# Out-projection of seven batches by seven block products on pairs of token chunks, in an attention and mixture kernel

## The chip, the cores and the metric

One core of a Trainium2 chip. The time is the device time of one execution in microseconds (us), and a median is over the runs of one kernel on one chip. All runs told here are fast: the granted TensorE clock was 0.95 to 1.0 as a mean over the run. The profile is of one of these executions; its span is some 2 us shorter than the timed value.

## The reference

```python
def sm_attn(qq, kk, vv):                       # softmax attention, 8 heads of 64
    s = scale * np.matmul(qq, kk.transpose(0, 1, 3, 2))
    ...
    return np.matmul(a, vv)
p_packed = sm_attn(p, k, v)                    # 32 packed queries per head
x = sm_attn(q, p_packed, p_packed)             # 8 batches x 576 tokens x 512
h = x @ w_in                                   # 512 x 2048
out = (h * np.cos(h)) @ w_out                  # 2048 x 512: the out-projection
```

## The kernel before

The kernel works batch by batch. A batch has a short *head* (scores, softmax sums, normalising to `a2n`) and a long *slot* of sixteen hidden blocks `h_mm`, which make `gT`. The out-projection of the batch before is the *filler*: its matmuls are handed out in small portions between the other work of TensorE (`fill(n)`). A batch has four chunks of 128 tokens, and what is left of two batches makes one joint chunk. Names used below: a *bank* is a piece of the memory that TensorE writes its results to, and another engine has to empty it before TensorE can use it again; `vp` is a batch's `v`, reordered by one copy on GpSimd; `PPW` is the packed attention result times `w_in`, which VectorE or ScalarE casts out of its banks; `rs` is a scaling of two numbers per partition on VectorE that the softmax needs.

```python
def h_mm(b, fc):
    ...                                   # 4 matmuls of 288 columns into one psA buffer (of 3)
    ACT.activation(out=csv, in_=ps, func=AF.Sin, bias=PI_HALF)
    V.tensor_tensor(out=gT..., in0=ps, in1=csv, op=ALU.mult)
    ...                                   # fc 7 and 15: GpSimd copies the rest tokens to `joint`

def out_gen(b):                           # one chunk = 16 matmuls of 512 columns into one bank
    groups = [(0, 1), (2,), (3,)] if b == 0 else [(c,) for c in range(n_chunks(b))]
    for grp in groups:
        pss = {c: O.tile([128, DM], FP32, name="ot", tag="ot") for c in grp}   # two banks
        ...
                    w = joint[b // 2][:, fc, :] if c == 4 else gT[b][:, fc, c * 128:(c + 1) * 128]
                    nc.tensor.matmul(pss[c], w, w_out_bf[:, fc, :], ...)
                    if fc == NFC - 1:
                        copy(out_eng[...], osb, pss[c])       # VectorE or ScalarE, then the store
```

The softmax here doesn't subtract the row's maximum and nothing guards it: scores larger than these inputs give would overflow.

## Time and profile before

| | before |
|---|---|
| time, median of 4 runs | 248.2 us (248.0 to 248.84) |
| span of the profiled run | 246.8 us |
| TensorE / VectorE / ScalarE / GpSimd busy | 94% / 67% / 68% / 23% |
| heads of batches 3 to 7 | 8.6 to 8.8 us |
| slots of batches 3 to 6 | 16.6 to 19.6 us |

The stages are cut at ScalarE's table loads: it loads the exponential's table when a head begins and the sine's when a slot begins. The lines themselves are in the prediction below. What to take from them is that TensorE has hardly an idle moment from the first batch on, and that no other engine is near its limit.

### The profile page before, as it was taken

How to read it: one execution, taken by the hardware profiler on the slowest of the kernel's cores; microseconds unless marked ns; L12 is line 12 of the kernel's file. 1: busy time of each engine (PE TensorE's matmuls, PEld its weight loads, DVE VectorE, ACT ScalarE, POOL GpSimd, SP SyncE). 2: the span in 40 equal slices, each digit the busy share in tenths (PEclk: the TensorE clock that was granted, in tenths of full speed). 3: DMA queues.
4: the chain of work that ended last, by engine and by line, in shares of the span. 5: the costliest groups of instructions: out<-in, count | busy, mean ns of one | idle time of the engine just before them, and what ended most of it. 6: DMA issues, size and time to landing. Idle time of an engine off the chain costs nothing.

```text
span 246.8 us, 5023 instructions
## 1 busy us (share of the span) xinstructions
PE 233.2 (94%) x1996; PEld 130.9 (53%) x2029; DVE 165.2 (67%) x248; ACT 169.0 (68%) x282; POOL 57.7 (23%) x70
## 2 busy tenths in 40 slices
PE   8788799999999999999999999999999999999993
PEld 3454374566545654565446554565456554665452
DVE  3549987677658776678767766678766684886110
ACT  2369799877576787888787776888778684873000
POOL 8342533240400355004503105030500100001000
PEclk9999999999999999999999999999999999999999
DMA  6999999999899999999999997999571113111133
GB/s 90 202 203 206 205 206 228 194 241 151 179 202 184 192 175 214 218 198 142 222 211 187 172 201 91 198 166 171 109 154 27 45 43 84 43 31 57 47 84 85
DMA packets 64231, 37.36 MB, mean 151 GB/s; under 512 B 36848, under 2 KB 59632, under 8 KB 64208
## 3 DMA queue, kind: packets, MB, share of 16 engines
q0 software_dynamic: 23152, 18.75, 50.0%
q1 hardware_dynamic: 40624, 18.09, 35.1%
q8 instruction: 16, 0.26, 0.4%
q10 hardware_dynamic: 432, 0.20, 0.4%
q14 instruction: 7, 0.06, 0.1%
HBM read 37.22 MB, written 9.44 MB: 189 GB/s over the span
## 4 chain that ended last, share of the span: by engine, by line
PE 78%; DMA 12%; issue 2%; DVE 2%; ACT 2%; POOL 2%; DVEq 0%; POOLq 0%
PE ot L309 46%; PE psA L256 21%; DMA vbf<-in_v_dram 10%; PE psA L207 3%; DMA a1T<-a 2%; PE psA L129 2%; PE psA L183 2%; DVE gT L263 2%; PE ot L295 1%; PE psA L233 1%; ACT cosT L260 1%; POOL vp L77 1%; ACT ppT L75 1%; POOL kbf L84 1%; PE ot L104 0%
## 5 line engine op out<-in xcount | busy, mean ns | idle before, releaser
L309 PE MATMUL ot<-w_out_bf,gT 128*128 128x512 bf16 x482 | 127.5, 379 | 2.0 <-issue 1.1
L263 DVE TENSOR_TENSOR gT<-psA,cosT 128x576 bf16<-128x576 f32 x128 | 93.8, 755 | 28.9 <-ACT cosT L260 28.2
L260 ACT ACTIVATE cosT<-psA 128x576 bf16<-128x576 f32 x128 | 82.4, 652 | 24.6 <-PE psA L256 22.1
L256 PE MATMUL psA<-a2n,PPW 128*128 128x288 bf16 x512 | 83.8, 286 | 1.6 <-DVE gT L263 0.4
L309 PEld LDWEIGHTS <-gT 128*128 128x128 bf16 x512 | 47.8, 98 | 43.4 <-issue 6.7
L256 PEld LDWEIGHTS <-PPW 128*128 128x128 bf16 x512 | 49.3, 98 | 34.6 <-issue 3.9
L77 DVE CAST PPW<-psA 128x1024 bf16<-128x1024 f32 (+1 forms) x23 | 26.9, 1175 | 11.6 <-PE psA L207 11.5
L267 POOL COPY joint<-gT 128x512 bf16<-128x512 bf16 x16 | 9.9, 616 | 82.5 <-DVE gT L263 82.5
L77 DVE COPY osb<-ot 128x512 f32<-128x512 f32 (+1 forms) x22 | 14.9, 678 | 17.5 <-PE ot L309 7.7
L77 POOL COPY vp<-vbf 96x3072 bf16<-96x3072 bf16 x7 | 19.3, 2751 | 6.3 <-DMA vbf<-in_v_dram 6.3
L75 ACT COPY osb<-ot 128x512 f32<-128x512 f32 (+1 forms) x15 | 8.5, 567 | 15.3 <-PE ot L309 10.6
L243 DVE SCALAR_TENSOR_TENSOR a2n<-a2u,r,lns 128x576 bf16<-128x576 bf16 x16 | 12.3, 812 | 7.3 <-ACT lns L241 7.3
L235 ACT ACTIVATE lns<-psA 128x576 f32<-128x576 f32 x16 | 10.1, 650 | 7.1 <-PE psA L233 6.5
L140 ACT ACTIVATE a<-psA 128x576 bf16<-128x576 f32 x16 | 10.3, 647 | 6.7 <-PE psA L129 6.7
L309 PE MATMUL ot<-w_out_bf,joint 128*128 128x512 bf16 x47 | 12.8, 379 | 0.1
L225 ACT ACTIVATE a2u<-psA,rs 128x576 bf16<-128x576 f32 x16 | 11.0, 737 | 1.4 <-PE psA L129 1.3
L75 ACT CAST ppT<-psA 64x128 bf16<-64x128 f32 x24 | 6.2, 260 | 7.0 <-DVE ppT L77 5.9
L207 PE MATMUL psA<-w_in_bf,ppT 64*32 64x512 bf16 x224 | 10.1, 380 | 0.0
L241 ACT ACTIVATE lns<-lns 128x576 f32<-128x576 f32 x16 | 10.0, 676 | 0.0
L347 PE MATMUL ot<-wz 128*128 128x512 bf16 x23 | 7.7, 468 | 1.4 <-DVE wz L358 1.2
L527 POOL COPY gate<-kT 1x1 bf16<-1x1 bf16 x3 | 0.5, 181 | 32.3 <-DMA kT<-kbf 32.3
L183 PEld LDWEIGHTS <-vp 96*128 96x128 bf16 x192 | 6.5, 98 | 2.3 <-issue 1.2
(73 smaller groups left out, 152.7 us busy)
## 6 DMA issues: line engine op xcount, KB each, us to landing
kbf<-in_k_dram POOLq DMA_DIRECT2D x8, 576.0 KB, 12.6
vbf<-in_v_dram POOLq DMA_DIRECT2D x8, 576.0 KB, 7.6
qbf<-in_q_dram POOLq DMA_DIRECT2D x8, 576.0 KB, 10.1
out_dram<-osb SPq DMA_DIRECT2D x24, 192.0 KB, 2.7
out_dram<-osb SPq DMA_DIRECT2D x22, 128.0 KB, 2.4
w_in_bf<-in_moe_w_in_dram POOLq DMA_DIRECT2D x4, 512.0 KB, 17.3
w_out_bf<-in_moe_w_out_dram POOLq DMA_DIRECT2D x4, 512.0 KB, 21.2
out_dram<-osb SPq DMA_DIRECT2D x26, 64.0 KB, 2.1
```

What stands on the lines that cost most here:

```text
L75: ACT.copy(out=out, in_=in_)
L77: eng.tensor_copy(out=out, in_=in_)
L140: ACT.activation(out=a1[b % 2][:, y, :, 0:TP].rearrange("p (e m) x -> p e m x", e=2), in_=ps[y][:, :, 0:HS].rearrange("p e (m x) -> p e m ...
L183: nc.tensor.matmul(ps[:, hp * 64:(hp + 1) * 64], vp[b][:, c, hp * 128:(hp + 1) * 128], a1T[b][0:TP, :, j, 32 * hp:32 * hp + 32], start=(j ...
L207: nc.tensor.matmul(ps[y][32 * x:32 * x + 32, :], ppT[b % 2][r, 2 * x + y, :], w_in_bf[r, x, n * 512:(n + 1) * 512], start=True, stop=True)
L225: ACT.activation(out=a2u[b][:, y].rearrange("p (e x) -> p e x", e=2), in_=ps[y][:, :, 0:HS], func=AF.Exp, scale=rs1[b][:, y:y + 1])
L235: ACT.activation(out=lns[b][:, y].rearrange("p (e x) -> p e x", e=2), in_=ps[:, :, 0:HS], func=AF.Ln)
L243: V.scalar_tensor_tensor(out=a2n[b][:, y], in0=a2u[b][:, y], scalar=r1[b][:, y:y + 1], in1=lns[b][:, y], op0=ALU.mult, op1=ALU.mult)
L256: nc.tensor.matmul(ps[:, e, 0:HS], PPW[b][:, y, fc * 128:(fc + 1) * 128], a2n[b][:, y, e * HS:(e + 1) * HS], start=(y == 0), stop=(y == 1))
L260: ACT.activation(out=csv, in_=ps[:, :, 0:HS], func=AF.Sin, bias=PI_HALF)
L263: V.tensor_tensor(out=gT[b][:, fc, :].rearrange("p (e x) -> p e x", e=2), in0=ps[:, :, 0:HS], in1=csv, op=ALU.mult)
L309: nc.tensor.matmul(pss[c], w, w_out_bf[:, fc, :], start=(fc == 0), stop=(fc == NFC - 1))
```

## The change

It means to save matmul time by a product scheme of the Strassen–Winograd kind. A pair of token chunks is a 2 x 2 block matrix (two chunks by even and odd hidden blocks), and `w_out` is another (two column halves by even and odd hidden blocks). Seven block products replace eight. The price is four block sums S of `gT` for each pair, four sums T of `w_out` once, and additions when the banks are emptied. GpSimd makes most S sums, VectorE the rest.

```diff
+    def T_sums(i, eng): ...                   # T0, T1, T3 on V, T2 on G, all in slot 1
+    def S_sums(b, p, eng, k0, k1, which=(0, 1, 2, 3)):
+        ...                                   # S1=A21+A22, S2=S1-A11, S3=A11-A21, S4=A12-S2
+            eng.tensor_tensor(out=out, in0=in0, in1=in1, op=op)
+    def pairs_gen(b):                         # 2 pairs x 7 products x 8 matmuls of 256 columns
+        ...                                   # two products share a bank; VectorE empties it by additions
+            return [(0, (1,)), (0, (2, 6)), (0, (7,)), (0, (4, 5)), (None, (3, 1)),
+                    (1, (2, 6)), (1, (7,)), (1, (4, 5)), (1, (3,))]
     def out_gen(b):
+        for j, i in joints_of(b):             # the joint chunk in halves, and FIRST
+            yield from joint_half(j, i, store_half(j))
+        yield from pairs_gen(b)
     ...
         for fc in range(NFC):                 # slot(s)
             h_mm(s, fc)()
+            if s > 1 and fc in (7, 11):
+                S_sums(s, 0, G, *((0, 4) if fc == 7 else (4, 6)))
     ...
+    def close(s):                             # between slot s and head s+1
+        S_sums(s, 0, V, 6, 8, (0, 1))
+        fill(1000)
+        S_sums(s, 0, V, 6, 8, (2, 3))
+        for k0 in (0, 4):
+            S_sums(s, 1, V if s == B - 1 else G, k0, k0 + 4)
+        set_filler(s)
```

Cut here: `PPW` in quarter tiles, smaller buffer counts, a2n's products moved behind a few fillers.

## The prediction

> **What bounds the kernel now.** I read the page's table of busy times first, then the chain that ended last, then that chain in order of time, then busy times by stretch. The stretches are cut at ScalarE's table loads: each batch has a short *head* (scores, softmax, normalising) and a long *slot* (sixteen hidden blocks, `h_mm`).
>
> ```profile
> PE 233.2 (94%) x1996; PEld 130.9 (53%) x2029; DVE 165.2 (67%) x248; ACT 169.0 (68%) x282; POOL 57.7 (23%) x70
> PE 78%; DMA 12%; issue 2%; DVE 2%; ACT 2%; POOL 2%; DVEq 0%; POOLq 0%
> ```
>
> TensorE is on 78% of the chain; the 12% of DMA is the load at the start. VectorE and ScalarE are two thirds busy, GpSimd one quarter: room that the change wants to spend.
>
> ```profile
> 224.00 4.32 PE ot L309 x20
> 228.37 10.74 PE ot L309 x49
> 239.16 3.67 PE ot L295 x32
> ```
>
> These pieces give the price of an out-projection matmul: 4.32/20 = 0.216 us with 512 columns; 3.67 us less the last one's own 0.27 us, over 31 gaps, is 0.1095 us with 256 columns, each with a new weight block. So halving the columns halves the pace, and the doubled weight loads stay hidden. The "379 ns" of the groups is latency, not pace.
>
> ```profile
> 119.40:128.10 8.70, 8.49 (x83) 3.86 (x84) 5.33 (x9) 6.53 (x13) 3.30 (x2) 1.00 1.28 216
> 128.10:147.60 19.50, 19.29 (x151) 11.62 (x152) 14.14 (x19) 14.56 (x24) 3.09 (x5) 1.00 1.06 191
> 147.60:156.50 8.90, 8.79 (x84) 3.94 (x85) 5.33 (x8) 6.52 (x13) 3.30 (x2) 1.00 0.71 114
> 156.50:173.10 16.60, 16.41 (x137) 10.25 (x138) 13.65 (x19) 14.04 (x24) 2.32 (x4) 1.00 0.94 172
> ```
>
> Head and slot of batch 4 (28.2 us, beside the out-projection of batch 3 with its joint chunk) and of batch 5 (25.5 us). After the length come TensorE, its weight loads, VectorE, ScalarE, GpSimd. TensorE leaves about 0.2 us idle per stretch; VectorE has 19 us of work in either batch, GpSimd 5.6 to 6.4.
>
> ```profile
> L263 DVE TENSOR_TENSOR gT<-psA,cosT 128x576 bf16<-128x576 f32 x128 | 93.8, 755 | 28.9 <-ACT cosT L260 28.2
> L77 DVE COPY osb<-ot 128x512 f32<-128x512 f32 x21 | 14.5, 690 | 14.6 <-PE ot L309 7.7 <-remote 6.2
> L77 DVE COPY osb<-ot 128x256 f32<-128x256 f32 x1 | 0.4, 424 | 2.9 <-PE ot L295 2.9
> L243 DVE SCALAR_TENSOR_TENSOR a2n<-a2u,r,lns 128x576 bf16<-128x576 bf16 x16 | 12.3, 812 | 7.3 <-ACT lns L241 7.3
> L77 POOL COPY vp<-vbf 96x3072 bf16<-96x3072 bf16 x7 | 19.3, 2751 | 6.3 <-DMA vbf<-in_v_dram 6.3
> L267 POOL COPY joint<-gT 128x512 bf16<-128x512 bf16 x16 | 9.9, 616 | 82.5 <-DVE gT L263 82.5
> ```
>
> These groups (shapes kept apart) price the new work: a VectorE pass over PSUM costs 0.69 us for 512 columns and 0.42 for 256. The two GpSimd copies give (2751 - 616)/(3072 - 512) = 0.83 ns an element and a fixed 0.19 us.
>
> **What the Trainium skill says.** "TensorE: Matmul & The Clock Gate", section Back-to-back issue gap, gives N/2.4 + 2.5 ns, 215.8 ns for 512 and 109 ns for 256 columns: the trace has 216 and 109.5. (The same section's 131 ns in a stream of 512-column matmuls is not what this trace has.) "GPSIMD Engine Reference", section 3.1, gives 4497 ns for a two-input `tensor_tensor` of 2048 fp32 elements: 2.2 ns each. The trace of before has no such instruction; if bf16 costs the same, which is an estimate, 512 elements take about 0.19 + 1.11 = 1.30 us and 256 about 0.75. "VectorE: DVE Perf Modes" (Mode 2×_1P) lets a two-source bf16 operation run two elements a cycle; no two-source bf16 operation of before shows it. I estimate 0.29 us for 256 elements and 0.42 for 512 (at 0.96 GHz, plus the 0.155 us that 755 ns leaves above 576 elements at one a cycle). "SBUF — State Buffer", section on the two sides, says that VectorE with two SBUF inputs and GpSimd reading SBUF exclude each other for a whole instruction; before has no pair of the kind at one time (the a2n products are 806 to 818 ns throughout), so no run here shows it yet.
>
> **The change part by part.**
>
> *TensorE.* A batch of 1 to 7 has two pairs. Before: 64 matmuls x 0.2155 = 13.79 us. After: 2 pairs x 7 products x 8 = 112 x 0.1095 = 12.26 us. 1.53 us saved, x 7 = 10.7. The three full joint chunks in halves cost 96 x 0.1095 - 48 x 0.2155 = 0.17 more. Net **10.5 us**, all on the bounding engine. By place, since joint halves move between batches: batch 2 loses 1.5 us, batch 3 1.5, batch 4 3.2, batch 5 gains 0.2, batch 6 loses 3.2, batch 7 gains 0.2, the end loses 1.5.
>
> *VectorE.* A pair's recombination is 256 (to m1), 512, 256, 512, 256, 256 columns: 4 x 0.42 + 2 x 0.69 = 3.06 us; in most slots the second pair's m1 goes to ScalarE (2.64). With the joint half's copy 0.42 and four block sums of 256 (1.16) that is 7.28 us, against three osb copies (2.07) that go. So 19.0 + 5.2 = 24.2 us in a batch that TensorE needs 25 to 25.7 us for: no longer idle by a third, but 95% full. In the slot (order of the built program, first to last hidden block): 11.6 for gT, one PPW cast 1.2, recombination 0.42 + 0.69 + 0.42: 14.35 us, against TensorE's 16 x 0.488 + 51 x 0.1095 + 1.3 (pp, ppw) = 14.7. In order, with three PSUM buffers, such a balance costs some waits. Once, in batch 1, three T sums of 2048 elements cost 3.7 us.
>
> *GpSimd.* Each batch gets eight sums of 512 (second pair), four of 512 and four of 256 (first pair): 12 x 1.30 + 4 x 0.75 = 18.6 us. With 6.4 us of today that is 25.0 us: **full**. And it is in order: vp of the next batch, copied at 149.0 just after the boundary today, stands behind 10.4 us of sums with one buffer in place of two, and pp needs it some 14.2 us after the boundary (161.8 against 147.6). I estimate 0.6 + 10.4 + 2.75 = 13.8 us: just in time.
>
> *Batch 2.* The first pair's sums of batch 1 stand on GpSimd behind a wait for kT (64.9 us before) and three loads, until 67.7, then the joint copy: they start at 68.3. The sum that product 6 needs for its steps 4 and 5 is there after 4 x 1.3 + 2 x 0.75 = 6.7 us, at 75. TensorE gets there 48 half steps into the batch, about 71.5 to 72. A wait of up to 3 us, where the change saves 1.5.
>
> *End.* 154 half matmuls (16.9 us) in place of 69 + 32 (18.4). But VectorE does the last second-pair sums there, 8 x 0.42 = 3.4 us, before it empties the bank of products 2 and 6, and there are two such banks: I estimate 0.8 us of waiting after some overlap.
>
> *PPW in quarters*, the smaller buffers and fewer vp and osb buffers save memory; I see no time in them but the vp wait.
>
> Sum: -10.5; batch 2 +2 (two thirds of the full wait, in case GpSimd is quicker); T sums in batch 1 +0.8; near-full VectorE and the exclusion, 0.45 in each of batches 3 to 6, +1.8; end +0.8. That is -5.1: **243.2 us**.
>
> **The rivals.**
> *All hidden*: TensorE stays the bound and the sums are free. For it: 5.7 of the 7.3 us of new VectorE work lie outside the span from first to last hidden block, in heads where it is idle for 40% today, and the second pair's sums are asked for late, in the slot. Against it: three engines at 95 to 100% in order. 237.9 us.
> *GpSimd becomes the bound*: if its sums cost 1.3 us and each exclusion adds to them (2.8 us of two-input VectorE work per batch, 2 x 0.81 + 4 x 0.29), a batch takes about 27 us in place of 25 to 25.7, pp waits for vp in each, and batch 2 ends 4 us later than before instead of 1.5 earlier. -10.5 + 4 x 1.6 + 5.5 = +1.4, nothing won: 248 to 250 us. For it: the sum of 25.0 us. Against it: the split gives VectorE just the last eighth of these sums, as a split measured to fit would.
> *VectorE becomes the bound*: a slot is then its 14.35 us plus waits for locks and banks, up to 1.3 us each at a2n, on the way to the first hidden block. About 1.5 us per batch: 245 to 246 us.
>
> **Range and chances.** The prize is certain (same pace, fewer columns); what is handed back hangs on the price of one GpSimd sum. At 0.9 us I get about 239, at 1.1 about 242, at 1.3 with locks 248. Hence 238.5 to 249. The threshold of faster is 243.4, about my centre: 0.5 faster, 0.44 same, 0.06 slower.
>
> **What would show it.** Right: L413 at 0.11 us pace with weight loads hidden; VectorE at some 85 to 90% and GpSimd at 75 to 95% of batches 3 to 6; TensorE still most of the chain, with new waits on GpSimd's S0 in batch 2. GpSimd sums of 512 well under 1 us would make the all-hidden rival right; pp waiting for vp in each slot makes the GpSimd rival right; gT waits before `h_mm` growing in each slot, with GpSimd idle, the VectorE one. A pace above 0.12 us per half matmul would make the whole gain wrong.

## The result, and the profile after

| | before | after |
|---|---|---|
| time, median of 4 runs | 248.2 us | **280.19 us** (279.15 to 281.33) |
| span of the profiled run | 246.8 us | 277.4 us |

The ratio is 1.129 (95% interval 1.123 to 1.134): **13% slower**, far outside the predicted range. Ratios here and below are the mean time of one kernel's fast runs over that of the other's from the same rounds, so they are not quite the ratio of the medians.

The first lines are the page's busy times and its chain of the work that ended last, for the changed kernel.

```profile
PE 236.2 (85%) x2407; PEld 172.4 (62%) x2413; DVE 223.2 (80%) x350; ACT 164.8 (59%) x278; POOL 166.8 (60%) x175
PE 14%; DVE 5%; POOL 3%; issue 2%; ACT 1%; DVEq 0%; ACTq 0%
```

TensorE fell from 94% to 85% busy, VectorE rose by 58 us, GpSimd by 109 us. The chain's shares add up to only 25%: it can be followed back no further than 203.9 us, so here it can't tell what bounds the kernel. The stages can:

| us | slot 1 | head 2 | slot 2 | head 3 | slot 3 | head 4 | slot 4 | head 5 | slot 5 | head 6 | slot 6 | head 7 | slot 7 to end |
|---|---|---|---|---|---|---|---|---|---|---|---|---|---|
| before | 19.67 | 12.64 | 19.11 | 8.63 | 16.60 | 8.62 | 19.58 | 8.84 | 16.60 | 8.62 | 19.50 | 8.60 | 36.99 |
| after | 23.61 | 13.81 | 20.70 | 13.18 | 17.15 | 12.56 | 18.12 | 12.58 | 18.08 | 12.61 | 18.04 | 12.40 | 41.55 |
| longer by | 3.9 | 1.2 | 1.6 | **4.6** | 0.6 | **3.9** | -1.5 | **3.7** | 1.5 | **4.0** | -1.5 | **3.8** | 4.6 |

The five heads 3 to 7 carry 20 us of the 30.6 us, slot 1 and the end 8.5 us. The slots of batches 3 to 6 are together shorter by about 1 us. The next lines are busy times by stretch of the changed kernel, for head 5 and slot 5 (length, then TensorE, its weight loads, VectorE, ScalarE, GpSimd, then the granted clock).

```profile
162.14:174.72 12.58, 9.98 (x113) 7.25 (x111) 11.32 (x17) 6.47 (x12) 12.26 (x12) 0.86 0.58 117
174.72:192.80 18.08, 17.36 (x176) 13.88 (x174) 16.29 (x24) 13.80 (x24) 9.55 (x13) 1.00 0.82 139
```

In the head VectorE is busy 11.3 of 12.6 us; in head 5 of before it was 5.3 of 8.8. The head's granted clock is 0.86. Why VectorE is so busy is in the groups of instructions, shapes kept apart (busy time and mean ns of one, then idle time before them).

```profile
L304 DVE TENSOR_TENSOR S<-gT 128x256 bf16<-128x256 bf16 x14 | 10.3, 738 | 0.7
L304 DVE TENSOR_TENSOR S<-gT,S 128x256 bf16<-128x256 bf16 x7 | 6.7, 963 | 0.0
L304 DVE TENSOR_TENSOR S<-S,gT 128x256 bf16<-128x256 bf16 x7 | 6.5, 926 | 0.2
L304 DVE TENSOR_TENSOR S<-gT 128x512 bf16<-128x512 bf16 x4 | 1.7, 418 | 0.0
L246 DVE SCALAR_TENSOR_TENSOR a2n<-a2u,r,lns 128x576 bf16<-128x576 bf16 x16 | 14.8, 958 | 0.0
L155 DVE TENSOR_SCALAR rs<-r 128x2 f32<-128x2 f32 x8 | 5.2, 644 | 0.3
L304 POOL TENSOR_TENSOR S<-gT 128x512 bf16<-128x512 bf16 x38 | 44.8, 1179 | 0.0
```

A VectorE sum of 256 elements takes 738 to 963 ns on average, while one of 512, made at the end where GpSimd is done, takes 418. So the smaller ones are mostly waiting. `rs` takes 644 ns on average; before it took 0.17 us in seven of its eight executions and 0.67 us in one. The wait is part of the instruction's record, so it reads as "busy". Taking 285 ns for a lone 256-element sum, 810 for a2n and 170 for rs (the runs below show all three), the excess is 14 x 0.45 + 7 x 0.68 + 7 x 0.64 + 16 x 0.15 + 8 x 0.47, some 22 us.

Head 6 in order of time shows how that reaches TensorE (start, duration, engine, line, and in brackets the idle time before it).

```profile
193.67 0.71 DVE L304 TENSOR_TENSOR S<-gT 128x256 bf16<-128x256 bf16 x1
194.20 1.19 POOL L304 TENSOR_TENSOR S<-gT 128x512 bf16<-128x512 bf16 x1
194.42 1.12 DVE L304 TENSOR_TENSOR S<-S,gT 128x256 bf16<-128x256 bf16 x1
...
195.47 0.68 DVE L372 TENSOR_TENSOR osb<-ot,u 128x512 f32<-128x512 f32 x1
...
196.07 0.94 DVE L372 TENSOR_TENSOR osb<-ot,osb 128x256 f32<-128x256 f32 x2
196.53 3.45 PE L323 MATMUL ot<-w_out_bf,joint 128*128 128x256 bf16 x16 [2.43 <-DVE osb L372]
...
202.40 1.13 DVE L155 TENSOR_SCALAR rs<-r 128x2 f32<-128x2 f32 x1
```

VectorE runs in order. Two block sums stand before the additions that empty the last banks of the batch before. The second sum ends 0.15 us after the GpSimd sum that it met (194.42 + 1.12 against 194.20 + 1.19): it waited for that one's end. TensorE stands still 2.43 us for the bank, and then the sixteen joint matmuls take 3.45 us in place of 1.9: the clock has fallen. Two more such sums follow (until 199.05 us), then a PPW cast, a copy out of a bank, a second cast, and rs. Head 3 has the same wait of 2.43 us, but the sixteen matmuls after it take 1.91 us and the clock of the whole head is 1.00; there TensorE waits 0.99 and 0.77 us for VectorE later on, and the head is the longest of the five. So the fallen clock is not what makes the heads long.

### The profile page after: what moved, and what is told of

Same layout as the page of the kernel before. It is cut to its first block, busy times and chain, and to the rows that moved or that the text cites. A ratio compares the mean times of both kernels' runs of the same rounds, so it can differ in the third digit from the quotient of the medians.

```text
span 277.4 us, 6071 instructions
## 1 busy us (share of the span) xinstructions
PE 236.2 (85%) x2407; PEld 172.4 (62%) x2413; DVE 223.2 (80%) x350; ACT 164.8 (59%) x278; POOL 166.8 (60%) x175
## 5 line engine op out<-in xcount | busy, mean ns | idle before, releaser
L270 DVE TENSOR_TENSOR gT<-psA,cosT 128x576 bf16<-128x576 f32 x128 | 92.9, 753 | 18.6 <-ACT cosT L267 16.3
L304 POOL TENSOR_TENSOR S<-gT 128x512 bf16<-128x512 bf16 (+1 forms) x52 | 54.1, 1041 | 0.0
L413 PE MATMUL ot<-T,S 128*128 128x256 bf16 x336 | 48.7, 273 | 0.3 <-DVE m L80 0.2
L413 PEld LDWEIGHTS <-S 128*128 128x128 bf16 x448 | 43.2, 98 | 9.0 <-issue 2.7
L413 PEld LDWEIGHTS <-gT 128*128 128x128 bf16 x336 | 31.9, 98 | 15.1 <-issue 7.4
L413 PE MATMUL ot<-w_out_bf,gT 128*128 128x256 bf16 x224 | 33.2, 273 | 4.6 <-DVE osb L372 4.6
L323 PE MATMUL ot<-w_out_bf,joint 128*128 128x256 bf16 x128 | 21.7, 340 | 10.2 <-DVE osb L372 10.0
L304 POOL TENSOR_TENSOR S<-S,gT 128x512 bf16<-128x512 bf16 (+1 forms) x26 | 27.1, 1044 | 2.0
L304 POOL TENSOR_TENSOR S<-gT,S 128x512 bf16<-128x512 bf16 (+1 forms) x26 | 26.9, 1033 | 0.0
L413 PE MATMUL ot<-T,gT 128*128 128x256 bf16 x112 | 16.8, 272 | 1.9 <-DVE osb L372 1.9
L237 ACT ACTIVATE lns<-psA 128x576 f32<-128x576 f32 x16 | 10.1, 650 | 13.2 <-PE psA L235 13.1
L345 PE MATMUL ot<-w_out_bf,gT 128*128 128x512 bf16 x60 | 16.4, 379 | 0.4 <-issue 0.3
```

What stands on the lines that cost most here:

```text
L237: ACT.activation(out=lns[b][:, y].rearrange("p (e x) -> p e x", e=2), in_=ps[:, :, 0:HS], func=AF.Ln)
L270: V.tensor_tensor(out=gT[b][:, fc, :].rearrange("p (e x) -> p e x", e=2), in0=ps[:, :, 0:HS], in1=csv, op=ALU.mult)
L304: eng.tensor_tensor(out=out, in0=in0, in1=in1, op=op)
L323: nc.tensor.matmul(ps, joint[b // 2][:, fc, :], w_out_bf[:, fc, cols], start=(fc == 0), stop=(fc == NFC - 1))
L345: nc.tensor.matmul(pss[c], gT[b][:, fc, c * 128:(c + 1) * 128], w_out_bf[:, fc, :], start=(fc == 0), stop=(fc == NFC - 1))
L413: nc.tensor.matmul(tile_[:, i], lhs[:, kp, :], rhs[:, kp, :], start=kp == 0, stop=kp == 7)
```

## The experiments

Twelve kernels were run. The changed function is named in each diff; lengths of stages are again cut at the table loads. This table is the reading of all traces, one profiled execution for each kernel. How well such a length repeats is seen in experiment 11: its program is that of the change up to head 4, and yet its slot 1 is 1.8 us and its head 3 1.1 us longer. A difference of that size in one of these two stages of a single trace shows nothing.

| us | slot 1 | head 2 | slot 2 | head 3 | slot 3 | head 4 | slot 4 | head 5 | slot 5 | head 6 | slot 6 | head 7 | slot 7 to end |
|---|---|---|---|---|---|---|---|---|---|---|---|---|---|
| 1 no sums | 20.10 | 17.73 | 20.76 | 9.85 | 17.16 | 9.09 | 17.07 | 9.09 | 17.07 | 9.09 | 17.07 | 8.86 | 39.26 |
| 2 no GpSimd sums | 25.02 | 13.26 | 20.70 | 11.42 | 17.16 | 10.68 | 17.07 | 10.68 | 17.07 | 10.68 | 17.35 | 9.79 | 41.05 |
| 3 VectorE sums | 22.00 | 20.98 | 22.15 | 14.83 | 20.62 | 15.07 | 20.59 | 14.37 | 20.19 | 14.76 | 19.80 | 13.02 | 43.37 |
| 4 empty first | 23.62 | 14.85 | 20.83 | 14.04 | 17.19 | 13.93 | 17.08 | 13.92 | 17.08 | 13.89 | 17.07 | 13.27 | 40.91 |
| 5 one pair | 22.06 | 21.76 | 19.25 | 10.33 | 17.51 | 10.33 | 18.32 | 10.41 | 18.31 | 10.40 | 18.32 | 8.90 | 38.79 |
| 6 GpSimd sums | 21.86 | 15.00 | 21.08 | 10.19 | 18.62 | 9.09 | 19.37 | 9.09 | 19.37 | 9.10 | 19.36 | 8.85 | 42.62 |
| 7 no sums, joint last | 20.19 | 13.17 | 20.19 | 9.33 | 17.16 | 9.84 | 18.04 | 9.42 | 18.04 | 9.41 | 18.05 | 8.85 | 37.89 |
| 8 GpSimd sums, joint last | 22.01 | 21.39 | 20.65 | 10.05 | 19.92 | 10.01 | 19.51 | 10.15 | 19.51 | 10.15 | 21.20 | 8.86 | 43.34 |
| 9 mended | 25.63 | 13.18 | 20.10 | 9.14 | 17.15 | 9.09 | 18.24 | 9.10 | 17.69 | 9.09 | 17.29 | 8.85 | 40.21 |
| 10 one pair, mended | 23.72 | 12.69 | 19.63 | 8.54 | 17.78 | 8.48 | 18.04 | 8.65 | 17.97 | 8.65 | 17.97 | 8.40 | 39.01 |
| 11 warm | 25.41 | 13.74 | 20.71 | 14.30 | 17.15 | 12.26 | 18.40 | 12.28 | 18.39 | 12.27 | 18.42 | 11.79 | 41.50 |
| 12 four batches | 20.02 | 12.67 | 19.03 | 9.72 | 20.25 | 9.09 | 17.26 | 9.10 | 17.67 | 9.09 | 17.26 | 8.80 | 38.87 |

### 1. No sums at all (wrong result)

```diff
     def S_sums(...):
+        return
     def T_sums(i, eng):
+        return
-            S1, S2, S3, S4 = (S[b, p][:, i] for i in range(4))
+            S1, S2, S3, S4 = (A_blk(b, 2 * p + i // 2, i % 2, 0, 8) for i in range(4))
+            T = [B_blk(i % 2, i // 2) for i in range(4)]
```

> Changed kernel with no block sums at all (blocks of gT and w_out stand in for S and T, so the result is wrong on purpose); the seven products and all recombination on VectorE stay. Theory A (the block sums, and the waits between VectorE and GpSimd that they bring, cost the time): most of the 32 us go, 240 to 246 us. Rival B (half-width products with two PSUM banks and the recombination on VectorE cannot keep TensorE fed, whoever does the sums): 260 us or more.

Measured: 256.57 us against 248.71 for before on that chip, ratio 1.031 (1.028 to 1.035). It lies between the two expectations. The sums and all that hangs on them cost 280.2 - 256.6 = 23.6 us. But the rest still costs 8 us, where 10.5 us were to be saved. The largest part of that is head 2, at 17.7 us:

```profile
67.53 0.62 POOL L274 COPY joint<-gT 128x512 bf16<-128x512 bf16 x1
...
68.21 0.39 PE L325 MATMUL ot<-w_out_bf,joint 128*128 128x256 bf16 x2 [3.37 <-POOL joint L274]
```

The joint chunk stands first in the list now, and its last copy on GpSimd comes late, behind loads that are issued in order. In the change itself the same copy is made at 68.36 us, but TensorE waits only 0.17 us for it, because slot 1 ended 3.7 us later. So slot 1 and head 2 have to be read together: 32.3 us before, 37.4 us in the change, 37.8 us here, without any sums.

### 2. No S sums on GpSimd (wrong result)

```diff
     def S_sums(b, p, eng, k0, k1, which=(0, 1, 2, 3)):
+        if eng is G:
+            return
```

The blocks that are not summed are replaced by blocks of `gT`.

> Only GpSimd's S sums are left out (gT stands in for these blocks, wrong on purpose); VectorE's four S sums of the last eighth, all T sums and the recombination stay. Theory A in its narrow form (VectorE's two-input instructions wait for GpSimd's): VectorE's S sums fall from 0.71 to 1.24 us to 0.29 us, the a2n products from up to 1.4 to 0.81, rs from 1.13 to 0.17, the gap before the joint half from 2.4 to about 1.2 us: 246 to 254 us. If instead VectorE's own share of the sums is what holds it, little changes: over 268 us.

Measured: 267.22 us, ratio 1.075 (1.070 to 1.079), between the two expectations. 13 us came back, fewer than expected; heads 4 to 6 are 1.9 us shorter than in the change. What is left in each head (10.7 us against 9.1 without sums) is visible in head 5:

```profile
159.29 0.29 DVE L306 TENSOR_TENSOR S<-gT 128x256 bf16<-128x256 bf16 x1
...
160.00 2.81 POOL L80 COPY vp<-vbf 96x3072 bf16<-96x3072 bf16 x1
...
161.58 1.38 DVE L306 TENSOR_TENSOR S<-gT 128x256 bf16<-128x256 bf16 x1
```

The same instruction takes 0.29 us with GpSimd idle and 1.38 us beside GpSimd's copy of vp, and it ends with that copy (160.00 + 2.81 = 162.81; 161.58 + 1.38 = 162.96). So it is not sums against sums: GpSimd's copy of vp holds VectorE up as well.

### 3. All sums on VectorE

```diff
-                S_sums(s, 0, G, *((0, 4) if fc == 7 else (4, 6)))
+                S_sums(s, 0, V, *((0, 4) if fc == 7 else (4, 6)))
-            S_sums(s, 1, V if s == B - 1 else G, k0, k0 + 4)
+            S_sums(s, 1, V, k0, k0 + 4)          # likewise T2 and batch 1's first pair
```

> Right result: all S and T sums on VectorE, none on GpSimd. Exclusion gone, but some 5 us more VectorE work in each batch (12 x 0.42 to 0.43 us), which makes VectorE the bound with about 28 us a batch. Theory A: VectorE's two-input work at its bare price, 258 to 270 us, a little faster than the changed kernel in spite of the added work. If exclusion costs little: slower than the changed kernel, 290 us or more.

Measured: 306.62 us, ratio 1.232 (1.228 to 1.236), a correct result, and the rival's side. No VectorE sum waits for a GpSimd sum now (one in each head still meets the copy of vp), 512 elements cost 0.42 us, and yet it is 26 us slower than the change. In each head VectorE's stream has two sums, the bank's additions and then ten sums, and only then the casts and copies that TensorE waits for. Head 5:

```profile
181.90 1.91 PE L323 MATMUL ot<-w_out_bf,joint 128*128 128x256 bf16 x16 [1.40 <-DVE osb L372]
...
188.32 0.60 PE L413 MATMUL ot<-w_out_bf,gT 128*128 128x256 bf16 x4 [2.02 <-DVE osb L80]
```

So the theory that only the exclusion costs falls: the sums' own time, **where** it stands in VectorE's order, costs as well. This run alone doesn't separate the amount of VectorE's work from its order: VectorE is busy 11.5 of the 14.4 us of head 5.

### 4. Banks emptied before the sums

```diff
-        S_sums(s, 0, V, 6, 8, (0, 1))
         fill(1000)
-        S_sums(s, 0, V, 6, 8, (2, 3))
+        S_sums(s, 0, V, 6, 8)
```

> Right result: at the end of a slot VectorE first empties the banks of the last pair and then does its four S sums, in place of two sums before. Theory A: TensorE's gap of 2.4 us before the joint half shrinks below 1 us, the clock no longer falls (the half took 3.45 us in place of 1.75), some 2.5 to 3.5 us less in each of batches 4 to 7 and at the end: 263 to 270 us. If the order does not matter because the waits only move to the sums' readers: 276 us or more.

Measured: 284.01 us, ratio 1.141 (1.137 to 1.146), 4 us slower than the change and on the side of the second expectation. The wait for the bank is gone (2.43 to 0.46 us), but the next consumer of VectorE waits instead:

```profile
166.31 1.91 PE L323 MATMUL ot<-w_out_bf,joint 128*128 128x256 bf16 x16 [0.46 <-DVE osb L372]
...
172.00 0.41 PE L209 MATMUL psA<-w_in_bf,ppT 64*32 64x512 bf16 x8 [2.97 <-DVE PPW L80]
```

Between the two VectorE makes its four sums, from 166.7 to 170.8 us. Reordering within VectorE moves the wait and doesn't remove it. As long as those sums are slow, something on TensorE's way stands behind them.

### 5. One pair only

```diff
-            begin(1)
-            return [(0, (1,)), ..., (1, (3,))]
+            return [(0, (1,)), (0, (2, 6)), (0, (7,)), (0, (4, 5)), (0, (3,))]
     # out_gen: pairs_gen(b), then chunks 2 and 3 in 512 columns, then the joint halves
     # close: S_sums(s, 0, V if s == B - 1 else G, 6, 8); T2 on VectorE
```

> Only the first pair of chunks of each batch goes through seven products; chunks 2 and 3 are again 512 columns wide, the joint chunk comes last in two halves, all sums of the first pair are on GpSimd (VectorE in the last batch) and all four T sums on VectorE. TensorE is asked for half of the predicted saving, 5 us less than before. Theory A (the loss is VectorE waiting for its SBUF sums while GpSimd sums, plus the joint chunk put first): almost none of VectorE's instructions then meet a GpSimd sum, so 242 to 248 us. Rival B (the block products themselves cost, their recombination fills VectorE and stalls the slots): half of what the kernel without sums lost, 250 to 256 us. The result should be correct.

Measured: 269.86 us, ratio 1.086 (1.084 to 1.088). Far above both expectations, and worse than both pairs without sums (experiment 1). Head 2 takes 21.8 us: GpSimd sums batch 1's pair only after slot 1, and the products wait for it. And in the later heads two numbers hold everything up:

```profile
166.95 2.74 POOL L80 COPY vp<-vbf 96x3072 bf16<-96x3072 bf16 x1
...
168.56 1.17 DVE L155 TENSOR_SCALAR rs<-r 128x2 f32<-128x2 f32 x1
...
170.37 0.81 PE L411 MATMUL ot<-T,gT 128*128 128x256 bf16 x6 [1.55 <-DVE osb L372]
```

`rs` ends as the copy of vp ends (169.7 us), the bank's addition stands behind it, and TensorE waits 1.55 us.

### 6. All S sums on GpSimd, all T sums on VectorE

```diff
-        S_sums(s, 0, V, 6, 8, (0, 1))
+        S_sums(s, 0, V if last else G, 4 if last else 6, 8)     # last: batch 7
         fill(1000)
-        S_sums(s, 0, V, 6, 8, (2, 3))
     ...
-  (8, lambda: (T_sums(0, V), T_sums(2, G))),
+  (8, lambda: T_sums(0, V)), ... (11, lambda: T_sums(2, V)),
```

> The change with every S sum on GpSimd (the last batch's late ones on VectorE) and every T sum on VectorE in slot 1, where GpSimd then sums nothing. VectorE runs no SBUF-to-SBUF sum while GpSimd sums, except a2n and the small reciprocal scaling. Theory A (VectorE standing still behind GpSimd's sums is the loss): slot 1 loses its 4 us of wait, the heads fall from 12.6 us to about 10, and the time to 256 to 264 us. Rival B (the S blocks come too late whoever makes them, or GpSimd becomes the bound): 275 us or more, with TensorE waiting for S.

Measured: 269.12 us, ratio 1.083 (1.080 to 1.086), correct, between the two expectations. 11 us came back, less than the 16 to 24 expected, but the heads confirm the theory sharply. Heads 4 to 7 are **9.09, 9.09, 9.10 and 8.85 us, the same as with no sums at all** (9.09 and 8.86), though GpSimd now makes more sums than in the change. Head 4 and slot 4 by stretch:

```profile
129.80:138.90 9.10, 8.58 (x114) 6.74 (x113) 7.07 (x14) 6.48 (x12) 8.92 (x12) 1.00 0.75 136
138.90:158.30 19.40, 17.24 (x174) 13.60 (x172) 17.16 (x23) 13.82 (x24) 17.09 (x18) 1.00 0.96 164
```

And from the timeline, TensorE's wait at the start of slot 5:

```profile
170.37 0.40 PE L263 MATMUL psA<-a2n,PPW 128*128 128x288 bf16 x2 [1.22 <-DVE a2n L246]
```

Taking four VectorE sums out of the head removed 3.5 us of it. Experiment 2 tells what these 3.5 us are: without GpSimd's sums the head is 1.9 us shorter; the other 1.6 us are what the four sums cost with GpSimd not summing, about 1.15 us of their own time (4 x 0.29) and a wait for the copy of vp. What is left is in the slots (19.4 us against 17.1): a2n, the last VectorE instruction of that kind, now has a mean of 1284 ns where 810 is its own time, and vp comes 0.43 us late because GpSimd, busy 26.0 of 28.5 us here, is in order too. Slot 1 got 1.75 us shorter by not summing T on two engines at once: it is 21.9 to 22.1 us in the four traces that do so (3, 5, 6, 8) and 23.6 to 25.4 us in the four with both engines (the change, 2, 4, 11). Head 2 is 1.2 us longer, though, so the two stages together gain only 0.6 us. In the changed kernel that had looked like this:

```profile
55.91 4.05 POOL L290 TENSOR_TENSOR T<-w_out_bf 128x2048 bf16<-128x2048 bf16 x1
...
56.98 4.07 DVE L290 TENSOR_TENSOR T<-w_out_bf 128x2048 bf16<-128x2048 bf16 x1
...
61.77 0.41 PE L263 MATMUL psA<-a2n,PPW 128*128 128x288 bf16 x2 [3.79 <-DVE gT L270]
```

A sum of 1.21 us (so in this experiment) took 4.07 us, and gT stood behind it.

### 7. No sums, joint chunk last (wrong result)

```diff
     # experiment 1, and in out_gen:
+        yield from pairs_gen(b)
         for j, i in joints_of(b):
             yield from joint_half(j, i, store_half(j))
-        yield from pairs_gen(b)
```

> The kernel without any sums (wrong result on purpose, as in the first experiment, 256.6 us) with the one difference that the joint chunk's halves come last in each batch's list of products in place of first. Theory A (of what that kernel loses, the largest part is the joint chunk standing first: in head 2 it waited 3.4 us for GpSimd's copy and then ran at the lower clock): 250 to 252.5 us, head 2 back to 16 to 17 us from 20.1. Rival B (the loss is spread over the slots and heads, from VectorE's recombinations): 255 to 257 us.

Measured: 254.3 us, ratio 1.023 (1.021 to 1.025), between the two expectations: 2.3 us better than experiment 1, less than the 4 to 6.5 expected. Head 2 came back from 17.7 to 13.2 us, so its cause is shown. (The 20.1 us in the expectation are the length of slot 1, not of head 2.) But batches 4 to 6 lost 1.3 to 1.7 us each, so "joint first" is not wrong everywhere. The kernel without sums remains slower than before: slot 2 (20.2 us, VectorE busy 17.1) and the end (37.9) are longer.

### 8. All S sums on GpSimd, joint chunk last

The edits of experiments 6 and 7 together.

> All S sums on GpSimd and all T sums on VectorE as in the second kernel of this call, and the joint chunk last. Theory A (the two causes add): 3 to 6 us less than the second kernel of this call, 251 to 259 us. Rival B (with the joint chunk last, the products that need S come earlier and wait for GpSimd): no gain, or slower than that kernel.

Measured: 282.05 us, ratio 1.135 (1.132 to 1.139): 13 us **slower** than experiment 6, the rival's side. With the joint chunk last, TensorE comes to the S products earlier by the joint halves (1.75 us each by their pace) and waits for GpSimd:

```profile
L413 PE MATMUL ot<-T,S 128*128 128x256 bf16 x336 | 51.3, 279 | 6.3 <-POOL S L304 5.3
```

Head 2 alone is 6.4 us longer. The two fixes do not add: with the joint halves first, GpSimd has more time.

### 9. Mended: both pairs of batches 1 to 6

```diff
-        V.tensor_scalar(out=rs1[b], in0=r1[b], scalar1=scale, ...)
+        ACT.activation(out=rs1[b], in_=r1[b], func=AF.Copy, scale=scale)
     # all S sums on GpSimd; batch 1's first pair within slot 1; T sums on VectorE at fc 0, 1, 2, 4
     # second pair: two sums, then vp, then (a wait for a2n) the other six
+        G.tensor_copy(out=gate, in_=a2n[s][0:1, 1, 0:1])
+        S_sums(s - 1, 1, G, 4, 8, (0, 1)) ...
     # joint chunk of batch 1 last, of the others first; batch 7 in 512-column chunks
```

> Both pairs of batches 1 to 6 through seven products, with each wait that the runs so far showed taken away: all S sums on GpSimd and ordered so that none runs beside a2n or beside the small reciprocal scaling (which goes to ScalarE), the first pair's sums of batch 1 already in slot 1, the T sums on VectorE early in slot 1, the joint chunk of batch 1 last, batch 7 in whole 512-column chunks as before, since its sums have nothing to hide behind. Theory A (exclusion between the two engines, order and the last batch's sums are all of the loss): stage by stage as in the kernels without sums, heads 9.1 us, slots 17 to 17.5 us, the end as before, so 245 to 250 us, the kernel before again or slightly better, with the correct result. Rival B (something else in the sums costs time, such as memory traffic, or late S blocks): above 255 us.

Measured: 257.8 us, ratio 1.035 (1.033 to 1.038), correct: **22 us of the 32 us came back** with all sums of six batches still made (the profiled execution is the slowest of the five, 260.03 us). Some 18 us of them are in heads 3 to 7. By its number it lies on the rival's side, stage by stage mostly on that of theory A. Heads 3 to 7 are at 8.85 to 9.14 us, as with no sums, and slots 3 to 6 at 17.2 to 18.2 us, at most 1.2 us longer than with none. The total misses the 245 to 250 us because of two stages. Slot 1 is 25.6 us, longer than in the change: the four T sums were packed into its first five hidden blocks, and the fourth met the copy of vp.

```profile
53.84 2.75 POOL L80 COPY vp<-vbf 96x3072 bf16<-96x3072 bf16 x1 [2.92 <-DMA vbf<-in_v_dram]
...
54.80 2.86 DVE L290 TENSOR_TENSOR T<-w_out_bf,T 128x2048 bf16<-128x2048 bf16 x1
```

The other is the end, 40.2 us against 37.0, where TensorE waited 0.94, 0.33 and 1.04 us for VectorE's gT and bank additions in slot 7. Since many edits were made at once, this run shows what they do together, not each one's share.

### 10. Mended, one pair only

As experiment 9 without the second pair; the list of a batch is chunk 2, the pair, chunk 3, the joint halves.

> As the kernel above, but only the first pair of batches 1 to 6 goes through seven products; chunk 2 stands first in each batch's list (so GpSimd has time for the last quarter of the sums), then the pair, then chunk 3 and the joint halves. TensorE is asked for some 4.7 us less than before, GpSimd has only half of the sums. Theory A: the waits of the first one-pair kernel (9 us in head 2, 1.55 us in each head behind the reciprocal scaling) go, 243 to 248 us. Rival B (the recombinations on VectorE and their banks give it back): 249 to 256 us.

Measured: 254.3 us, ratio 1.022 (1.020 to 1.024), in the rival's range. Head and slot of batches 4 to 6 take 26.5, 26.6 and 26.6 us, together 79.8 us against 81.8 before. But in these three stages one joint half less is done than before, which moved to slot 7 (sixteen matmuls, 1.75 us by their pace), so hardly 0.3 us are won. Slot 1 is 4.1 us longer than before (the T sums again).

### 11. Extra matmuls in TensorE's wait

```diff
     def out_gen(b):
+        if b > 2 and joints_of(b):
+            ps = psa()
+            for _ in range(10):
+                nc.tensor.matmul(ps[:, 0, :], ident, w_out_bf[:, 0, :], start=True, stop=True)
```

> The change with ten extra 512-column matmuls whose result nobody reads, put on TensorE where it waits 2.4 us for a bank in heads 4 to 7 ahead of the joint half. Theory A (the granted clock falls because TensorE stood still, and the 16 matmuls after the wait take 3.45 us in place of 1.75 us for that reason): they come back to about 1.8 us, the time falls by 4 to 7 us to 273 to 276 us. Rival B (those matmuls are slow for another reason, their weight loads or the memory): they keep their 3.45 us and the time stays at 280 us or rises.

Measured: 280.76 us, ratio 1.127 (1.122 to 1.133), the same as the change, where the rival had it. Head 6:

```profile
197.71 2.32 PE L431 MATMUL psA<-w_out_bf,ident 128*128 128x512 bf16 x10 [0.79 <-ACT a2u L227]
199.87 1.91 PE L323 MATMUL ot<-w_out_bf,joint 128*128 128x256 bf16 x16
```

The same head by stretch:

```profile
195.60:207.90 12.30, 11.02 (x125) 7.89 (x124) 10.90 (x17) 6.49 (x13) 11.99 (x12) 1.00 0.55 109
```

Theory A is right on the mechanism: with TensorE kept busy the granted clock is 1.00 and the sixteen matmuls take 1.91 us in place of 3.45. And it is wrong on the time: head 6 fell from 12.61 to 12.27 us only. The low clock was conspicuous and cost next to nothing, and VectorE is busy 10.9 of its 12.3 us. Head 3 of the change, long without a fallen clock, says the same. The extra matmuls took 2.3 us of TensorE themselves, and the joint half began some 0.5 us later after the head's start than in the change, so this is no exact price of the clock.

### 12. Both pairs of batches 2 to 5 only

Experiment 9 with batches 1, 6 and 7 in 512-column chunks, VectorE and ScalarE by turns at the end, and the T sums on GpSimd in slot 1 and head 2.

> Seven products for both pairs of batches 2 to 5 alone, with the order of the mended kernel; batches 0, 1, 6 and 7 in whole 512-column chunks as before, so that neither slot 1 nor the end carries sums or recombinations; the four T sums on GpSimd in slot 1 and head 2, where no VectorE instruction of the locked kind runs. Theory A (TensorE still sets the pace where nothing waits, and the products save it up to 1.6 us per batch): slot 1, head 2 and the end are as before (19.7, 12.6 and 37.0 us), and batches 2 to 5 give 1.5 to 4 us together, 244.5 to 247 us. Rival B (the recombinations on VectorE and the banks take all of it back, as the mended kernels suggest, batch 2 above all): 248 to 251 us, no gain.

Measured: 253.81 us, ratio 1.020 (1.017 to 1.022). No gain: some 2% slower than before, and above both expectations. Slot 1, head 2 and slot 2 are as before within 0.4 us, as expected; so in this trace the four T sums on GpSimd cost next to nothing there. But the sums of batch 2 began late, since GpSimd waited for a load, and ran into its copy of vp and so into a2n:

```profile
103.55 2.74 POOL L80 COPY vp<-vbf 96x3072 bf16<-96x3072 bf16 x1
...
104.53 3.10 DVE L246 SCALAR_TENSOR_TENSOR a2n<-a2u,r,lns 128x576 bf16<-128x576 bf16 x2
```

Two products of 1.6 us together took 3.1 us, and TensorE waited for the first of them 1.65 us. Slot 3 is 3.7 us longer than before. The three later batches are the fairest measure of the idea: with head and slot they take 26.35, 26.77 and 26.35 us, 79.5 us against 81.8. Of these 2.3 us, 1.75 are the joint half that moved to slot 7 (the end is 1.9 us longer for it), so some 0.5 us are won in three batches. No version that was run beats the kernel before.

## Why the prediction was wrong

**Right: the pace of TensorE.** Half-width matmuls run at 0.11 us each (in experiment 1, 26 of them in 2.90 us from start to start of what follows), and the doubled weight loads stay hidden. But hardly any of the saving reached the time: without sums, head and slot of batches 4 to 6 take 26.16 us each, 78.5 us against 81.8 before, and 1.75 us of these 3.3 are the moved joint half. The prediction had 6.2 us for these three batches.

**The step that failed: "near-full VectorE and the exclusion, 0.45 in each of batches 3 to 6, +1.8".** Heads 3 to 7 grew by 3.7 to 4.6 us each, some 20 us, and 3.3 to 3.5 us of each, some 17 us, go when no sums are made (experiment 1). The prediction had the mechanism, quoted it from the skill and named its victims (four sums and two a2n products per batch). It then priced the wait as part of VectorE's *average load* and looked for the loss in the slots, with their gT. But in the head VectorE's sums stand in order between the slot's last gT and the additions that free TensorE's banks, GpSimd works almost without a pause there (12.3 of 12.6 us), and each of them waits for up to one whole GpSimd sum, 1.15 us. Experiment 6 shows this by its reverse: with those four sums on GpSimd, heads 4 to 7 are what they are without any sums. Of the 3.5 us, 1.9 us are due to GpSimd's sums and 1.6 us to the four sums with GpSimd not summing (experiment 2). That VectorE was "idle for 40%" in the heads was true of before, but the idle time was no free room: VectorE has to answer TensorE there when a bank is full.

**Misleading sign.** "VectorE at some 85 to 90%" came true: in head and slot of batch 5 it is busy 27.6 of 30.7 us, 90%. But part of that is waiting inside the record, so the sign stood for the failure and not for the forecast. GpSimd is at 71% there, under the 75 to 95% named. Before also had a hint: one rs, at 66.56 us, took 0.67 us in place of 0.17 while GpSimd issued loads. The prediction looked at a2n alone. (No run tests that one wait.)

**Mis-sized, but masked: the T sums, "+0.8".** Slot 1 grew by 3.9 us. The prediction counted 3.7 us of VectorE work and did not see that T0 and T2 are asked for at the same time on the two engines that exclude each other. But slot 1 and head 2 together are as long without any sums (37.8 us) as in the change (37.4), as the late joint copy holds head 2 up when slot 1 ends earlier. So what the T sums cost in the change alone stays open. Where the joint chunk of batch 1 stands last, slot 1 is 3.5 us longer with four T sums on VectorE (experiment 10 against 7); with all four on GpSimd, slot 1 and head 2 are as before within 0.4 us (experiment 12). These are readings of one trace each.

**Mis-sized: the end, "+0.8" beside -1.5.** Slot 7 to the end grew by 4.6 us. The wait that was priced came as estimated: 0.79 us, behind the eight second-pair sums of 0.42 us. The others had no term: 2.19 us for the bank behind two first-pair sums (one of them 0.71 us beside GpSimd's joint copy), and 0.94 and 0.33 us for gT and a bank in slot 7.

**Failed as well: "The prize is certain (same pace, fewer columns)".** No term stood for what the products cost apart from their sums, and experiments 1 and 7 show it: without any sums the kernel is still 8 and 5.7 us slower than before. What the traces show of it is a joint chunk put first and waiting for a late copy (4.6 us in head 2, experiment 1 against 7), 0.46 us in each head for the bank that VectorE empties by two additions instead of one copy, 0.23 us in each slot, and slot 2 filled by VectorE (17.1 of 20.2 us). ScalarE, which before emptied 14 of the 512-column banks, empties 3 after (and seven of 256); the additions of the products are all on VectorE. Of the 1.5 us per batch that the pace promises, about 0.5 us is left even with no sums ((3.3 - 1.75)/3).

**Wrong: GpSimd full, vp just in time, batch 2 waiting for S.** A sum of 512 elements took 1.18 us (estimate 1.30), one of 256 took 0.67 (0.75), so 12 x 1.18 + 4 x 0.67 = 16.8 us per batch in place of 18.6, in a batch that had become longer. GpSimd was not the bound. What the prediction hung its range on, the price of one GpSimd sum, was not the error: at 1.18 us its own scale lies between 242 and 248 us. VectorE's bare prices, 0.29 and 0.42 us, were right.

**The rivals.** "VectorE becomes the bound" was the nearest in cause, at 245 to 246 us, but it put the loss at a2n and in gT in the slots and sized it at 1.5 us per batch. "All hidden" and "GpSimd becomes the bound" fell. No rival let VectorE's waits in the heads add up along its order, and so the range left no room for the 32 us.

**Where the 32 us went**, as far as it is shown: 23.6 us with the sums (experiment 1), of which some 17 us in heads 3 to 7. The other 8 us, and the 10.5 us that were to be saved, went to the structure of the products, the joint chunk's place and the end included. In experiment 9, 22 us are back while the sums of six batches are still made, so most of the loss was waits and order, not work; but batch 7 and the joint chunk of batch 1 were changed there too, so not all of the 22 us need be part of the 23.6. How much of experiment 9's gain is due to each of its edits stays open, as does a remainder of some 0.3 us per batch in experiment 1 (1.0 us lost, 0.46 and 0.23 us of it in waits that the timeline shows).

## What to carry to other kernels

Moving work to idle engines is priced by what stands behind it in each engine's order, not by the engine's busy share; ask of each added instruction which consumer comes next in that stream. When two engines exclude each other for whole instructions, a short instruction on one costs the rest of a long one on the other, so keep all of that work on one of the two, or keep the long ones away from the short ones. A fallen clock beside a wait can be a mere symptom, as it was here: ask first whether TensorE is what sets the length of the stage.

## What the Trainium skill lacked or had wrong

- "SBUF — State Buffer", section Who interferes with whom, states the exclusion, and the runs agree with it. It does not say what a stream of GpSimd instructions does to a VectorE that meets it: here VectorE got its turn at the end of the current GpSimd instruction, a 256-element sum in heads 3 to 7 taking 0.71 to 1.24 us in place of 0.29, while GpSimd's own 512-element sums rose only from 1.154 us (experiment 9, few collisions) to 1.179 us, and to 1.24 us in experiment 6, where the long a2n products meet them. Nor does it warn that the record of the waiting instruction counts the wait as busy, so that VectorE looked 80% busy.
- The same section counts `tensor_scalar` among those that can take both ports. The runs add how small such an instruction can be: 2 fp32 elements per partition waited until 1.17 us had passed, against 0.17 us alone.
- "TensorE: Matmul & The Clock Gate", section HAM oscillation — how this bites in real kernels, warns of idle gaps above some 3.4 us. Here the clock had fallen after waits of 2.43 to 2.50 us in heads 4 to 7: sixteen 256-column matmuls then took 3.40 to 3.48 us in place of 1.9. But in head 3 they took 1.91 us after the same 2.43 us, as they did after 1.40 us (experiments 2 and 3; in 3 the clock fell later in the head, after two more waits of 0.74 and 2.02 us), so the length of one wait doesn't decide it alone. The section has no figure for such shorter gaps.
- "GPSIMD Engine Reference", section 3.1, gives 4497 ns for a two-input operation of 2048 fp32 elements and no bf16 figure. In bf16 the runs show 4.05 us for 2048, 1.15 to 1.18 us (1.24 us in experiment 6) for 512 and 0.67 us for 256 elements.
